# First two batches interleaved, a new order in both sweeps, and new places for the first tiles of pass B

## The chip, the cores and the metric

One core of one Trainium2 chip runs the whole program. The metric is the device time of one execution in microseconds (us); lower is better. TensorE (PE) multiplies matrices into PSUM, VectorE (DVE), ScalarE (ACT) and GpSimd (POOL) work on tiles in SBUF, and SyncE (SP) issues all the DMAs, in one queue and in order. Each engine executes its own list of instructions in order and waits on semaphores for the others.

## The reference

Three layers over 8 batches of 576 rows follow each other: a linear attention, a mixer with a ReLU, and a gated unit with a tanh GELU.

```python
kv = einsum('bhsd,bhse->bhde', k, v); o = einsum('bhsd,bhde->bhse', q, kv)      # 8 heads of 64
x  = o / sqrt(mean(o*o) + 1e-6) * g_norm                                          # heads joined: 576 x 512
u  = x + (x^T @ U @ V)^T                                                          # rank 32 over the rows
z  = u + relu(u @ w_ch1) @ w_ch2                                                  # 512 -> 2048 -> 512
h  = gelu(z @ w_in); a, v = h[..., :512], h[..., 512:]
out = z + (a * (w_sg @ layernorm(v) * g_ln + b_sg)) @ w_out
```

## The kernel before, in words

Every product of fp32 values is made of three products of float32r tiles (`three`, L319): a value is split into a high tile (an ACT copy) and a low tile (a DVE or POOL subtraction). Weights come from DRAM as 64-bit pairs and are turned into fp32 first (`convert`, L95): two ACT instructions, three DVE instructions and one POOL addition for each, and then the two of the split.

**The first sweep** goes over the batches. For a batch, `att_kv` (K) multiplies keys and values of a pair of heads, `put_kv` copies the four results into the block diagonal tile `kvbd`, `att_x` (X0 to X4) multiplies the queries with it in five chunks of rows, `att_root` and `att_norm` normalize on DVE, `att_t` (T0 to T4) multiplies with U, and `att_u` (D0 to D3) transposes, adds the rank-32 part, writes u to DRAM and splits it. `ch1` (U) is one unit of the product u @ w_ch1 for the first six of the sixteen 128-wide columns of the hidden layer: 12 matmuls of 288 columns, 12 such units for a batch. PERIOD (L503) is written out by hand and says in which order PE does the units of batch b, K of batch b+2, and X, T, D of batch b+1; ahead of the first period stands a preamble (L445 to L501) that does all of attention for batch 0 and K for batch 1. `cook_1` and `cook_2` prepare the other ten columns' weights in the periods 1 to 5, after the units 4, 6 and 9 of a period.

**The second sweep** (`Unit`, L554) makes those ten columns in a Strassen-like form with seven products for a block of 1024 rows (five blocks). Each product ends in an ACT or DVE instruction that reads its PSUM tile (`keep`, `result`); `after` (L606) puts the next block's loads, sums and splits (`split_t`) between them.

**Pass B** reads relu(y) back (`load_y`, L695: a DMA, an ACT relu to `yh`, a DVE instruction to `yl`) and multiplies it with w_ch2 (`ch2`); each step takes one tile `yr`. The third layer follows.

PE's order is written by hand. The other engines' order is made by a scheduler from the order of the program and a priority (a counter, which `later(n)` raises by n), except where `behind` keeps two instructions in program order. A tile's place is set by pool and tag: a tag with `bufs=2` alternates between two places, and a new tile waits until the old one's readers are done. The preamble's keys and values have two places (`kvm`, `kvr`), so the loads of pairs 2 and 3 wait for K of pairs 0 and 1. The pool `cp` holds the five prepared weights c0 to c4, each written by `cook_2` in the periods 1 to 5.

Of the kernel before, what the change touches and what calls it, by code (L numbers as in the profile page):

```python
# [12 lines left out]
F32 = mybir.dt.float32  # L13
F32R = mybir.dt.float32r
# [7 lines left out]

B, H, S, D = 8, 8, 576, 64
DM, DFF, RANK = 512, 2048, 32
EH = 512
P = 128
NP = H // 2
# [31 lines left out]
def tile_kernel(ctx: ExitStack, tc: tile.TileContext, kvm, kvr, qt, gcol, uv, w12,  # L59
# [102 lines left out]
    kv_t, q_t = {}, {}  # L162

    def load_kv(b, p):
        m = ap.tile([P, 4, 2 * P], F32, tag="kvm", bufs=2, name="kvm")
        r = ap.tile([S - 4 * P, 2 * P], F32, tag="kvr", bufs=2, name="kvr")
        nc.sync.dma_start(m, kvm[b, p])
        nc.sync.dma_start(r, kvr[b, p])
        kv_t[b, p] = (m, r)

    def load_q(b, p):
        q = ap.tile([P, S], F32, tag=f"q{p}", name=f"q{p}")
        nc.sync.dma_start(q, qt[b, p])
        q_t[b, p] = q
# [32 lines left out]
    def cook_2(i):  # L207
# [8 lines left out]
        for o, x in ((slice(0, 2), a[:, 0:2]), (slice(2, 3), a[:, 3:4]), (slice(3, 7), s)):  # L216
            behind(nc.scalar.activation(c[:, 0, o], x, AF.Copy))
            behind(nc.vector.tensor_sub(c[:, 1, o], x, c[:, 0, o].bitcast(F32)))

    at_s = {}  # L220

    def att_kv(b, ps):
        if ps[0] == 0:
            at_s["kv", b] = pm.tile([P, NP, D], F32, tag="ar", bufs=4, name="kvps")
        acc = at_s["kv", b]
        for p in ps:
            m, r = kv_t.pop((b, p))
            for c in range(NC):
                src = m[:, c] if c < 4 else r
                for j in range(2):  # L230
                    mm(acc[j * D:(j + 1) * D, p, :], src[:, j * D:(j + 1) * D],
                       src[:, P + j * D:P + (j + 1) * D], start=(c == 0), stop=(c == NC - 1))
# [7 lines left out]
    def att_x(b, c):  # L240

        n = rows(c)
        if c == 0:
            at_s["ss", b] = ap.tile([P, NC, H], F32, tag="ss", name="ss")
            nc.gpsimd.memset(at_s["ss", b][64:, 4], 1.0)
        ps = pm.tile([P, H, D], F32, tag="ar", bufs=4, name="xps")
        for p in range(NP):
            mm(ps[:n, 2 * p:2 * p + 2, :], q_t[b, p][:, c * P:c * P + n], kvbd[:, p, :],  # L248
               start=True, stop=True)
        xn = ap.tile([P, H, D], F32, tag=f"xn{c}", name="xn")  # L250
        sq = ap.tile([P, H, D], F32, tag="sq", name="sq")
        nc.scalar.activation(sq[:n], ps[:n], AF.Square)
        nc.scalar.activation(xn[:n], ps[:n], AF.Copy)
        nc.vector.tensor_reduce(at_s["ss", b][:n, c], sq[:n], AX.X, ALU.add)
        at_s["x", b, c] = xn

    def att_root(b):
        ss = at_s.pop(("ss", b))
        y, t = (ap.tile([P, NC, H], F32, tag=i, name=i) for i in ("ny", "nt"))
        a, y2, t2 = (i.rearrange("p w h -> p (w h)") for i in (ss, y, t))  # L260
        nc.vector.tensor_scalar(a, a, 1.0 / D, EPS, ALU.mult, ALU.add)
        in_turn(rsqrt(y2, t2, a))
        at_s["y", b] = y
# [178 lines left out]

    nu = NC * RANK
    cut = nu + HS
    for p in range(2):  # L445
        load_kv(0, p)
    nc.gpsimd.memset(kvbd, 0.0)
    make_identity(nc, ident)
    for p in range(2):
        att_kv(0, [p])  # L450
        load_kv(0, p + 2)
    for p in range(NP):
        load_q(0, p)
    for p in range(2, NP):
        att_kv(0, [p])
    put_kv(0)
    uvr = [slot(8 + h, [w, 2], I32, "uv") for h, w in enumerate((cut, HS))]
    for h in range(2):
        nc.sync.dma_start(uvr[h].rearrange("p n k -> p (n k)"), uv[:, 2 * cut * h:2 * cut + 2 * HS * h])
    nc.sync.dma_start(g, gcol)  # L460
    for f in range(2):
        load_w(f, 0)
    for p in range(2):
        load_kv(1, p)
    for f in range(2, 4):
        load_w(f, 0)
    for c in range(NC):
        att_x(0, c)
    for p in range(NP):
        load_q(1, p)  # L470
    tmp_u = next_tmp()[:, :nu]
    in_turn(convert(uvr[0][:, :nu], tmp_u))
    store_u(tmp_u)
    att_root(0)
    att_norm(0, (0, 1))
    tmp_v = [next_tmp()[:, :HS] for _ in range(2)]
    for h, (r, t) in enumerate(zip((uvr[0][:, nu:], uvr[1]), tmp_v)):
# [2 lines left out]
    for cs in ((0, 1), (2, 3), (4,)):  # L480
        if cs[0]:
            att_norm(0, cs)
        for c in cs:
            att_t(0, c)
    for p in range(2):
        att_kv(1, [p])
        load_kv(1, p + 2)
    split_w(0)
    split_w(1)
    for d in range(ND):  # L490
        att_u(0, d)
    for p in range(2, NP):
        att_kv(1, [p])
    put_kv(1)
    for p in range(2):
        load_kv(2, p)
    for f in range(4, NA):
        load_w(f, 0)
    for f in range(2, NA):
        split_w(f)  # L500
    flush()  # L501

    PERIOD = "X0 X1 X2 X3 U U X4 U U K0 U K1 U T0 T1 U T2 T3 U T4 U K2 U K3 U U D0 D1 D2 D3".split()  # L503
    for b in range(B):
        n, n2 = (i if i < B else None for i in (b + 1, b + 2))
        i = 0
        if n is None:
            at.close()
            px["xa"] = xa = pha.enter_context(tc.tile_pool(name="xa", bufs=1, side="right", reuse_waits="tile"))
            first_block()  # L510
        for s in PERIOD:
            c = int(s[1:] or 0)
            if s[0] == "U":
                ch1(b, i)
                i += 1
                if 1 <= b <= NI and i in (4, 6, 9):
                    if i < 9:
                        cook_1(b - 1, i // 2 - 2)
                    else:
                        cook_2(b - 1)  # L520
                if b < NI and i in (10, 11):
                    load_w(NA + 2 * b + i - 10, 0)
            elif s[0] == "K" and n2:
# [82 lines left out]
    def after(j, i, p):  # L606


        if j + 1 < len(BLOCKS):
            if 1 <= i < 4:  # L610
                at_ = done[j] = done.get(j, -1) + 1
                if at_ == 0:
                    load_blocks(j + 1)
                elif at_ in (6, 8, 10):
                    sums(j + 1, {6: "T1", 8: "T2", 10: "T3"}[at_])
                elif at_ in (12, 13):
                    split_t(j + 1, {12: "T1", 13: "B11"}[at_])
            if i == NI - 1 and p != 4 and p != 2:
                w = {5: "B22", 1: "T2", 3: "T3", 6: "B21", 7: "T4"}[p]
                if w == "T4":  # L620
                    sums(j + 1, w)
                split_t(j + 1, w)
            if j + 2 < len(BLOCKS) + 1 and p == 4 and i < 4:
                f = 4 * j + i
                if f == 0:
                    load_w(0, 1, 18)
                split_w2(f)
                if f + 1 < NF:
                    load_w(f + 1, 1, 18)
        elif p == 4 and i == 0:  # L630
            flush()
# [40 lines left out]
    p2["rw"] = ph1.enter_context(tc.tile_pool(name="rw", bufs=1, side="right", reuse_waits="tile"))  # L672
    bp = ph1.enter_context(tc.tile_pool(name="bp", bufs=1, side="left", reuse_waits="tile"))
    pm1 = ph1.enter_context(tc.tile_pool(name="pm1", bufs=1, space=PSUM, reuse_waits="tile"))
    tmps[:] = [bp.tile([P, DM], F32, tag=f"tmp{i}", name=f"tmp{i}") for i in range(2)]

    HOMES = (8, 9, 10, 11, 12, 13, 0, 1, 2, 3, 4, 5)
    wio_raw, wio = {}, {}
# [14 lines left out]
        nc.sync.dma_start(zt[b], ud[b])  # L693

    def load_y(j, i):  # L695
        y = bp.tile([P, 2, BT], F32, tag="y", bufs=3, name="yr")
        nc.sync.dma_start(y, yd[j][:, 2 * i:2 * i + 2])
        yh = bp.tile([P, 2, BT], F32R, tag="yh", bufs=2, name="yh")
        yl = bp.tile([P, 2, BT], F32R, tag="yl", bufs=2, name="yl")
        nc.scalar.activation(yh, y, AF.Relu)  # L700
        nc.vector.scalar_tensor_tensor(yl, y, 0.0, yh.bitcast(F32), ALU.max, ALU.subtract)  # L701
        for k in range(2):
            ys[j, 2 * i + k] = yh[:, k], yl[:, k]
# [328 lines left out]
```

## Time and profile before

| | us |
|---|---|
| median of 3 runs (1418.52 to 1425.31) | 1422.9 |
| the profiled execution | 1419.69 |
| its span, first to last instruction | 1417.7 |
| PE busy (8050 matmuls) | 1353.7, 95% |
| DVE busy | 768.2, 54% |
| ACT busy | 544.8, 38% |
| POOL busy | 280.4, 20% |
| mean granted TensorE clock | 0.985 |

How to read it: PE is the engine that has the most to do, so what counts is where PE has nothing to do, and where a matmul takes longer than elsewhere. In the page's 40 slices PE has 5, 8, 8 and 8 tenths or more in the first ones (35 us each), 7 in the slice around 570 us, and 8 or 9 in nearly all others.

### The profile page before, as it was taken

To read this page: it belongs to the slowest core of one execution; us is meant where nothing else is said; L and a number is where in the kernel's file an instruction comes from. 1 tells how busy PE (TensorE), PEld (TensorE's weight loads), DVE (VectorE), ACT (ScalarE), POOL (GpSimd) and SP (SyncE) were. 2 spreads that over 40 slices of the span, in tenths; PEclk is the share of its full clock that TensorE was granted. 3 is DMA by queue.
4 is the path that set the end of the run, shared out by engine and by line. 5 is a ranking of instruction groups with operands and counts; after the bars stand their busy time and mean duration, and the time that the engine had idled before them with its cause. 6 is when DMAs were issued, how large, how long until landed. Compare 5 with 4: busy or idle time off the path is not lost.

```text
span 1417.7 us, 20709 instructions
## 1 busy us (share of the span) xinstructions
PE 1353.7 (95%) x8050; PEld 1180.6 (83%) x8050; DVE 768.2 (54%) x1373; ACT 544.8 (38%) x920; POOL 280.4 (20%) x268
## 2 busy tenths in 40 slices
PE   5889999999999899699999999999999999999998
PEld 3788888888778788588888888888999999999998
DVE  3746666646566653232223232556775775865864
ACT  3756666654444442221212121444432423333321
POOL 1400000000110110200000000326253543533332
PEclk8899999999999999899999999999999999999999
DMA  7666665445666677834454543741020110211001
GB/s 247 205 190 209 204 213 184 148 144 184 213 229 226 213 259 258 310 93 130 130 170 157 170 140 120 245 134 57 1 68 18 51 50 18 68 34 34 34 17 51
DMA packets 86929, 199.43 MB, mean 141 GB/s; under 512 B 12208, under 2 KB 33456, under 8 KB 85040
## 3 DMA queue, kind: packets, MB, share of 16 engines
q1 hardware_dynamic: 86832, 198.12, 42.0%
q8 instruction: 63, 1.03, 0.3%
q14 instruction: 34, 0.28, 0.1%
HBM read 126.00 MB, written 72.09 MB: 140 GB/s over the span
## 4 chain that ended last, share of the span: by engine, by line
PE 76%; DVE 6%; DMA 6%; ACT 3%; issue 2%; POOL 1%; SPq 1%; DVEq 0%; ACTq 0%; POOLq 0%
PE acc L321 9%; PE acc L322 9%; PE acc L320 9%; PE uso L883 8%; PE uso L904 5%; PE uso L795 4%; PE c L320 3%; PE c L321 3%; PE c L322 3%; PE y L320 2%; PE y L322 2%; PE y L321 2%; PE xps L248 2%; DMA zl<-zd 2%; PE v L320 2%
## 5 line engine op out<-in xcount | busy, mean ns | idle before, releaser
L320 PE MATMUL acc<-yh,w 128*128 128x512 f32 x576 | 225.5, 392 | 10.3 <-ACT yh L700 10.3
L701 DVE SCALAR_TENSOR_TENSOR yl<-yr,yh 128x1024 fp32r<-128x1024 f32 x72 | 89.4, 1241 | 258.4 <-ACT yh L700 258.1
L321 PE MATMUL acc<-yl,w 128*128 128x512 f32 x576 | 225.6, 392 | 0.6 <-DVE yl L701 0.5
L322 PE MATMUL acc<-yh,w 128*128 128x512 f32 x576 | 225.3, 391 | 0.0
L700 ACT ACTIVATE yh<-yr 128x1024 fp32r<-128x1024 f32 x72 | 76.4, 1061 | 284.8 <-PE acc L322 271.8
L320 PEld LDWEIGHTS acc<-yh,w 128*128 128x128 f32 x576 | 108.8, 189 | 32.9 <-ACT yh L700 10.5
L321 PEld LDWEIGHTS acc<-yl,w 128*128 128x128 f32 x576 | 108.7, 189 | 24.2 <-DVE yl L701 1.5
L322 PEld LDWEIGHTS acc<-yh,w 128*128 128x128 f32 x576 | 108.8, 189 | 22.5
L320 PE MATMUL c<-uh,w 128*128 128x288 f32 x384 | 118.0, 307 | 1.8 <-ACT y L337 1.3
L321 PE MATMUL c<-ul,w 128*128 128x288 f32 x384 | 114.0, 297 | 0.8 <-DVE ul L317 0.8
L322 PE MATMUL c<-uh,w 128*128 128x288 f32 x384 | 113.6, 296 | 0.0
L795 PE MATMUL uso<-zh,wio 128*128 128x288 f32 x512 | 94.2, 298 | 1.2 <-DVE g2u L803 1.2
L904 PE MATMUL uso<-gh,wio 128*128 128x288 f32 x512 | 93.1, 296 | 0.0
L108 POOL TENSOR_TENSOR tmp<-tmp,raw 128x512 int32<-128x512 int32 x22 | 33.6, 1528 | 270.4 <-DVE tmp L107 256.0
L320 PE MATMUL y<-T,c 128*128 128x512 f32 (+1 forms) x200 | 75.5, 378 | 9.6 <-DVE y L568 9.4
L108 POOL TENSOR_TENSOR tmp<-tmp,wior 128x512 int32<-128x512 int32 x12 | 15.7, 1306 | 345.8 <-DVE tmp L107 300.8
L904 PEld LDWEIGHTS uso<-gh,wio 128*128 128x128 f32 x512 | 78.0, 189 | 2.3 <-issue 0.2
L795 PEld LDWEIGHTS uso<-zh,wio 128*128 128x128 f32 x512 | 76.4, 188 | 3.8 <-PE uso L883 1.8
L320 PEld LDWEIGHTS c<-uh,w 128*128 128x128 f32 x384 | 72.7, 189 | 5.5 <-ACT y L337 1.5
L322 PE MATMUL y<-T,c 128*128 128x512 f32 (+1 forms) x200 | 74.7, 373 | 0.0
L321 PEld LDWEIGHTS c<-ul,w 128*128 128x128 f32 x384 | 72.7, 189 | 2.3 <-DVE ul L317 1.2
L321 PE MATMUL y<-T,c 128*128 128x512 f32 (+1 forms) x200 | 74.5, 372 | 0.0
(178 smaller groups left out, 2963.5 us busy)
## 6 DMA issues: line engine op xcount, KB each, us to landing
yr<-yd SPq DMA_DIRECT2D x72, 512.0 KB, 3.7
yd<-y SPq DMA_DIRECT2D x92, 256.0 KB, 3.2
kvm<-kvm_dram SPq DMA_DIRECT2D x32, 512.0 KB, 4.4
raw<-w_dram SPq DMA_DIRECT2D x32, 512.0 KB, 4.4
q<-qt_dram SPq DMA_DIRECT2D x32, 288.0 KB, 5.2
ud<-ut SPq DMA_DIRECT2D x32, 288.0 KB, 2.1
z<-ud SPq DMA_DIRECT2D x8, 1152.0 KB, 6.4
out_dram<-ot SPq DMA_DIRECT2D x31, 288.0 KB, 2.1
```

Source lines behind the costliest of these rows:

```text
L108: yield behind(nc.gpsimd.tensor_add(t, t, low))
L248: mm(ps[:n, 2 * p:2 * p + 2, :], q_t[b, p][:, c * P:c * P + n], kvbd[:, p, :], start=True, stop=True)
L320: mm(ps, ah, bh, start=start, stop=False, **kw)
L321: mm(ps, ah, bl, start=False, stop=False, **kw)
L322: mm(ps, al, bh, start=False, stop=stop, **kw)
L700: nc.scalar.activation(yh, y, AF.Relu)
L701: nc.vector.scalar_tensor_tensor(yl, y, 0.0, yh.bitcast(F32), ALU.max, ALU.subtract)
L795: mm(ps[:, e, :HS], a[:, s], c[:, halves[e]], start=(d == 0 and i == 0), stop=(d == ND - 1 and i == 2))
L883: mm(ps[:, e, :HS], a[:, s], w[:, halves[e]], start=(c == 0 and i == 0), stop=(c == NC - 1 and i == 1))
L904: mm(ops[d][:, e, :HS], a[:, s], c[:, f, halves[e]], start=(f == 0 and i == 0), stop=(f == ND - 1 and i == 2))
```

## The change

It has six parts, told in the order of the program.

1. The five places of `cp` are allocated at the start as `spare` tiles. Keys and values of the pairs 2 and 3 of batches 0 and 1 land in `spare[2]` and `spare[3]`, the raw weights of the columns 0 to 5 in `spare[0]` and `spare[1]`, and batch 0's normalized rows and small tiles live in `spare[4]`. All eight loads of batch 0 and its queries are now issued without a wait for PE.
2. The preamble does all four K of batch 0, X of batch 0, all four K of batch 1, and then T of batch 0 and X of batch 1 in turns. The root of batch 1 follows D of batch 0. The weights 2 to 5 are split later: 2 and 3 before the first period, 4 and 5 inside it.
3. The first period (FIRST) has no X any more.
4. In PERIOD, X4 comes after one unit instead of two, T2 after two units instead of one behind T1, T4 after two instead of one, and D after one instead of two.
5. In the second sweep the splits that stand at the end of a block get a priority that is later by 25.
6. In pass B three `yr` tiles and the two tiles `yx` (which hold `yh` and `yl` together) are allocated before and after the `tmp` tiles, at other places than before.

```diff
     def load_kv(b, p):
-        m = ap.tile([P, 4, 2 * P], F32, tag="kvm", bufs=2, name="kvm")
-        r = ap.tile([S - 4 * P, 2 * P], F32, tag="kvr", bufs=2, name="kvr")
+        if b < 2 and p >= 2:
+            x = spare[2 + b][:, (p - 2) * 5 * 2 * P:(p - 1) * 5 * 2 * P].rearrange("p (c k) -> p c k", c=5)
+            m, r = x[:, :4], x[:S - 4 * P, 4]
+        else:
+            m = ap.tile([P, 4, 2 * P], F32, tag="kvm", bufs=2, name="kvm")
+            r = ap.tile([S - 4 * P, 2 * P], F32, tag="kvr", bufs=2, name="kvr")
...
     def load_w(f, h, at_=None):
+        if f < NA and h == 0:
+            w_raw[f, h] = spare[f // 3][:, f % 3 * 2 * DM:(f % 3 + 1) * 2 * DM].bitcast(I32).rearrange(
+                "p (n k) -> p n k", k=2)
+            load_pairs(w_raw[f, h], w12[f], h)
+            return
...
-    for p in range(2):
+    for p in range(NP):
         load_kv(0, p)
+    for p in range(NP):
+        load_q(0, p)
...
-    for p in range(2):
-        att_kv(0, [p])
-        load_kv(0, p + 2)
...
+    att_kv(0, list(range(NP)))
     put_kv(0)
...
+    att_root(0)
     tmp_u = next_tmp()[:, :nu]
     in_turn(convert(uvr[0][:, :nu], tmp_u))
     store_u(tmp_u)
-    att_root(0)
+    att_kv(1, list(range(NP)))
+    put_kv(1)
     att_norm(0, (0, 1))
...
         for c in cs:
             att_t(0, c)
+        for c in cs:
+            att_x(1, c)
...
+    att_root(1)
+    for p in range(NP):
+        load_q(2, p)
+    split_w(2)
+    att_norm(1, (0, 1))
+    split_w(3)
+
+    PERIOD = "X0 X1 X2 X3 U X4 U U K0 U K1 U T0 T1 U U T2 T3 U U T4 U K2 U K3 U D0 D1 D2 D3".split()
+    FIRST = "U U U K0 U K1 U T0 T1 U U T2 T3 U U T4 U K2 U K3 U D0 D1 D2 D3".split()
...
+                if b == 0 and i in (1, 3, 5):
+                    if i < 5:
+                        split_w(4 + i // 2)
+                    else:
+                        flush()
...
-                if w == "T4":
-                    sums(j + 1, w)
-                split_t(j + 1, w)
+                with later(LATER):
+                    if w == "T4":
+                        sums(j + 1, w)
+                    split_t(j + 1, w)
...
+    y_at = [bp.tile([P, 2, BT], F32, tag="y", bufs=3, name="yr")]
     tmps[:] = [bp.tile([P, DM], F32, tag=f"tmp{i}", name=f"tmp{i}") for i in range(2)]
+    yx_at = {i: bp.tile([P, 2, 2, BT], F32R, tag=f"yx{i}", name="yx") for i in (1, 0)}
```

What this makes of the engines' lists shows at three places. The first is PE in the preamble, behind X of batch 0; `tp` is the result of T, `kvps` of K, `xps` of X, `ups` of D. Before, T stands alone:

```order
L248 MATMUL xps<-kvbd,q_171 64x128
L286 MATMUL tp<-xh,u_118 128x512
L288 MATMUL tp<-xl,u_118 128x512
...
L286 MATMUL tp<-xh,u_118 128x512
L231 MATMUL kvps<-kvm 64x64 x8
L231 MATMUL kvps<-kvr 64x64 x2
...
L310 MATMUL ups<-ident,xn 128x128 x2
```

The same place now (`spare_126` holds keys and values of batch 1, `q_260` a query tile of batch 1):

```order
L255 MATMUL kvps<-kvr 64x64 x2
L255 MATMUL kvps<-spare_126 64x64 x20
L310 MATMUL tp<-xh,u_118 128x512
L312 MATMUL tp<-xl,u_118 128x512
...
L272 MATMUL xps<-kvbd,q_260 128x128
L272 MATMUL xps<-kvbd,q_262 128x128
```

K of batch 1 has moved ahead of T of batch 0, and two chunks of X of batch 1 stand behind T0 and T1, two behind T2 and T3, and the last behind T4.

The second is DVE in a steady period (batch 1), from the low part of the last normalized chunk (`xh<-xn,xh 64x512`) to the copy into `kvbd`; `t` is the tile that D multiplies, `sums` and `c` belong to `cook_2`. Before:

```order
L277 TENSOR_TENSOR xh<-xn,xh 64x512
L292 TENSOR_TENSOR t_1224<-tp,t_1224 32x512
L212 TENSOR_TENSOR sums_1242<-pair_1096 128x256
L213 TENSOR_TENSOR sums_1242<-sums_1242,pair_1096 128x256
L214 TENSOR_TENSOR sums_1242<-pair_1096 128x256
L215 TENSOR_TENSOR sums_1242<-pair_1096,sums_1242 128x256
```

Now:

```order
L301 TENSOR_TENSOR xh<-xn,xh 64x512
L222 TENSOR_TENSOR sums_1221<-pair_1094 128x256
L223 TENSOR_TENSOR sums_1221<-sums_1221,pair_1094 128x256
L224 TENSOR_TENSOR sums_1221<-pair_1094 128x256
L225 TENSOR_TENSOR sums_1221<-pair_1094,sums_1221 128x256
L228 TENSOR_TENSOR c_1222<-pair_1094,c_1222 128x512
L228 TENSOR_TENSOR c_1222<-pair_1094,c_1222 128x256
L228 TENSOR_TENSOR c_1222<-sums_1221,c_1222 128x1024
L316 TENSOR_TENSOR t_1234<-tp,t_1234 32x512
```

The seven instructions of `cook_2` have moved ahead of the low part of `t`.

The third is DVE at the end of a block of the second sweep; `T` is a split tile of the next block, `y<-` a result that frees a PSUM tile. Before:

```order
L640 TENSOR_TENSOR w_4054<-tmp_3762,w_4054 128x512
L423 TENSOR_TENSOR T_4140<-tf,T_4139 128x1024
L423 TENSOR_TENSOR T_4153<-q,T_4152 128x1024
L568 TENSOR_TENSOR y<-y,s_4162 128x512
L568 TENSOR_TENSOR y<-y,m_4094 128x512
```

Now:

```order
L665 TENSOR_TENSOR w_4037<-tmp_3745,w_4037 128x512
L447 TENSOR_TENSOR T_4123<-tf,T_4122 128x1024
L592 TENSOR_TENSOR y<-y,s_4145 128x512
L592 TENSOR_TENSOR y<-y,m_4077 128x512
L447 TENSOR_TENSOR T_4136<-q,T_4135 128x1024
```

One split, T from q, has moved behind two results.

## Rows read from the trace of the kernel before

**Rows 1.** Busy time by stretch: us, engines (instructions), granted clock, DMA share, GB/s.
```profile
0.00:100.00 100.00, 73.71 (x582) 62.00 (x583) 52.93 (x102) 51.28 (x103) 18.65 (x24) 0.88 0.66 220
330.00:420.00 90.00, 84.81 (x359) 66.85 (x358) 51.93 (x68) 39.95 (x67) 11.12 (x7) 1.00 0.61 204
420.00:570.00 150.00, 140.11 (x693) 116.94 (x691) 80.79 (x116) 61.56 (x112) 14.05 (x9) 0.99 0.71 243
```
**Rows 2.** Timeline of SP and PE, the start: us, duration, instruction, idle before.
```profile
9.05 2.01 SPq L173 DMA_DIRECT2D q<-qt_dram  x4
...
16.66 5.86 PE L248 MATMUL xps<-kvbd,q 128*128 128x128 f32 x34 [0.46 <-DMA q<-qt_dram]
29.57 0.80 PE L286 MATMUL tp<-xh,u 128*128 128x512 f32 x1 [7.05 <-ACT xh L276]
51.81 3.81 PE L248 MATMUL xps<-kvbd,q 128*128 128x128 f32 x32 [1.01 <-ACT raw L103]
55.38 0.38 PE L320 MATMUL c<-uh,w 128*128 128x288 f32 x1
58.73 1.09 PE L248 MATMUL xps<-kvbd,q 128*64 128x128 f32 x8
73.53 0.50 PE L286 MATMUL tp<-xh,u 128*128 128x512 f32 x1 [3.44 <-ACT xh L276]
```
**Rows 3.** Timeline of DVE in the preamble: t, and the last low part of u.
```profile
40.08 0.70 DVE L292 TENSOR_TENSOR t<-tp,t 32x512 fp32r<-32x512 f32 x1 [1.66 <-ACT t L291]
51.74 0.76 DVE L317 TENSOR_TENSOR ul<-ut,uh 128x576 fp32r<-128x576 f32 x1
```
**Rows 4.** Busy time in a stretch of the preamble; the granted clock is the third last number.
```profile
30.00:39.00 9.00, 4.98 (x9) 2.30 (x8) 6.66 (x14) 3.68 (x9) 3.54 (x3) 0.50 0.01 4
```
**Rows 5.** Chain that ended last: start us, us; X0 of batches 2, 3 and 4.
```profile
94.47 0.91 PE xps L248 x8
131.56 3.57 PE xps L248 x32
168.09 3.57 PE xps L248 x32
```
**Rows 6.** PE's waits, 100 to 330 us (total, times, longest), and one wait.
```profile
PE tp L288 <- DVE xl L277: 6.7, 10, 0.9
...
151.62 0.50 PE L288 MATMUL tp<-xl,u 128*128 128x512 f32 x1 [0.84 <-DVE xl L277]
```
**Rows 7.** Timeline of DVE in a period: first and last of `cook_2`'s instructions.
```profile
156.62 0.42 DVE L212 TENSOR_TENSOR sums<-pair 128x256 f32<-128x256 f32 x1
159.31 1.23 DVE L218 TENSOR_TENSOR c<-sums,c 128x1024 fp32r<-128x1024 f32 x1 [0.19 <-ACT c L217]
```
**Rows 8.** Timeline of ACT and POOL: first and last instruction for one weight.
```profile
65.01 0.68 ACT L102 ACTIVATE tmp<-raw 128x512 f32<-128x512 f32 x1 [1.42 <-POOL w L125]
69.83 1.26 POOL L125 TENSOR_TENSOR w<-tmp,w 128x512 fp32r<-128x512 f32 x1 [0.74 <-ACT w L124]
```
**Rows 9.** Timeline of DVE and PE at two block ends of the second sweep.
```profile
485.71 2.32 DVE L423 TENSOR_TENSOR T<-tf,T 128x1024 fp32r<-128x1024 f32 x1
487.95 1.21 DVE L423 TENSOR_TENSOR T<-q,T 128x1024 fp32r<-128x1024 f32 x1
489.09 0.68 DVE L568 TENSOR_TENSOR y<-y,s 128x512 f32<-128x512 f32 x1
...
386.61 0.50 PE L320 MATMUL y<-T,c 128*128 128x512 f32 x1 [2.58 <-DVE y L568]
489.82 0.51 PE L320 MATMUL y<-T,c 128*128 128x512 f32 x1 [3.70 <-DVE y L568]
```
**Rows 10.** Timeline of SP, ACT and PE: the first tiles of pass B.
```profile
568.89 0.92 SPq L697 DMA_DIRECT2D yr<-yd  x2
576.17 1.06 ACT L700 ACTIVATE yh<-yr 128x1024 fp32r<-128x1024 f32 x1 [8.68 <-DMA yr<-yd]
577.28 0.79 PE L320 MATMUL acc<-yh,w 128*128 128x512 f32 x1 [10.25 <-ACT yh L700]
```

More of the change, by code (lines that the diff above doesn't have):

```diff
@@ L24 @@
 DM, DFF, RANK = 512, 2048, 32
+LATER = 25
 EH = 512
@@ L218, in cook_2, with xn_of, small @@
             behind(nc.vector.tensor_sub(c[:, 1, o], x, c[:, 0, o].bitcast(F32)))
+    spare = [cp.tile([P, 7 * DM], F32, tag=f"c{i}", name=f"spare{i}") for i in range(NI)]
+    def xn_of(b, c):
+        if b:
+            return ap.tile([P, H, D], F32, tag=f"xn{c}", name="xn")
+        return spare[4][:, c * DM:(c + 1) * DM].rearrange("p (h d) -> p h d", h=H)
+    def small(b, name, i):
+        if b:
+            return ap.tile([P, NC, H], F32, tag=name, name=name)
+        o = NC * DM + i * NC * H
+        return spare[4][:, o:o + NC * H].rearrange("p (c h) -> p c h", c=NC)
     at_s = {}
@@ L243, in att_x @@
         if c == 0:
-            at_s["ss", b] = ap.tile([P, NC, H], F32, tag="ss", name="ss")
+            at_s["ss", b] = small(b, "ss", 0)
             nc.gpsimd.memset(at_s["ss", b][64:, 4], 1.0)
@@ L249, in att_x @@
                start=True, stop=True)
-        xn = ap.tile([P, H, D], F32, tag=f"xn{c}", name="xn")
+        xn = xn_of(b, c)
         sq = ap.tile([P, H, D], F32, tag="sq", name="sq")
@@ L258, in att_root @@
         ss = at_s.pop(("ss", b))
-        y, t = (ap.tile([P, NC, H], F32, tag=i, name=i) for i in ("ny", "nt"))
+        y, t = (small(b, n, i) for i, n in ((1, "ny"), (2, "nt")))
         a, y2, t2 = (i.rearrange("p w h -> p (w h)") for i in (ss, y, t))
@@ L444, in tile_kernel @@
     cut = nu + HS
-    for p in range(2):
+    for p in range(NP):
         load_kv(0, p)
+    for p in range(NP):
+        load_q(0, p)
     nc.gpsimd.memset(kvbd, 0.0)
     make_identity(nc, ident)
-    for p in range(2):
-        att_kv(0, [p])
-        load_kv(0, p + 2)
[L452 to L455, printed above, removed]
+    att_kv(0, list(range(NP)))
     put_kv(0)
@@ L460, in tile_kernel @@
     nc.sync.dma_start(g, gcol)
-    for f in range(2):
-        load_w(f, 0)
-    for p in range(2):
+    for p in range(NP):
         load_kv(1, p)
-    for f in range(2, 4):
-        load_w(f, 0)
+    load_w(0, 0)
     for c in range(NC):
@@ L470, in tile_kernel @@
         load_q(1, p)
+    for f in range(1, NA):
+        load_w(f, 0)
+    att_root(0)
     tmp_u = next_tmp()[:, :nu]
@@ L484, in tile_kernel @@
             att_t(0, c)
+        for c in cs:
+            att_x(1, c)
     for p in range(2):
-        att_kv(1, [p])
-        load_kv(1, p + 2)
+        load_kv(2, p)
     split_w(0)
@@ L491, in tile_kernel @@
         att_u(0, d)
[L492 to L503, printed above, removed]
+    att_root(1)
+    for p in range(NP):
+        load_q(2, p)
[4 more added lines that the diff above has]
+    FIRST = "U U U K0 U K1 U T0 T1 U U T2 T3 U U T4 U K2 U K3 U D0 D1 D2 D3".split()
     for b in range(B):
@@ L510, in tile_kernel @@
             first_block()
-        for s in PERIOD:
+        for s in PERIOD if b else FIRST:
             c = int(s[1:] or 0)
@@ L695, in load_y @@
     def load_y(j, i):
-        y = bp.tile([P, 2, BT], F32, tag="y", bufs=3, name="yr")
+        y = y_at.pop() if y_at else bp.tile([P, 2, BT], F32, tag="y", bufs=3, name="yr")
         nc.sync.dma_start(y, yd[j][:, 2 * i:2 * i + 2])
-        yh = bp.tile([P, 2, BT], F32R, tag="yh", bufs=2, name="yh")
-        yl = bp.tile([P, 2, BT], F32R, tag="yl", bufs=2, name="yl")
+        k = i % 2
+        yx = yx_at.pop(k) if k in yx_at else bp.tile([P, 2, 2, BT], F32R, tag=f"yx{k}", name="yx")
+        yh, yl = yx[:, 0], yx[:, 1]
         nc.scalar.activation(yh, y, AF.Relu)
```

## The prediction

> **What bounds the kernel now.** I read the busy time by stretch first [rows 1]: PE is busy for 73.71 of the first 100 us, at a granted clock of 0.88, and for 84.81 of 90 and 140.11 of 150 us in the second sweep; nearly everywhere else it has no hole. So the end is set by PE, and a change can only gain what PE loses in holes, or what it loses at the lower clock. Then the waits and the timeline of PE in those stretches. In the preamble PE ends X of batch 0 and stands 7.05 us until the first normalized tile is there; it starts the first unit at 55.38 and stands 3.44 us again before T of batch 1 [rows 2]. From 30 to 39 us its granted clock is 0.50, the lower of its two levels (1.2 of 2.4 GHz) [rows 4]. In the steady periods the reader sees one repeated wait, of T2 and T3 for the low tile `xl`: 6.7 us in ten waits, five periods with two each, 0.84 the larger of a pair [rows 6]. In the second sweep PE stands 2.58 and 3.70 us at two block ends, for a DVE result that frees a PSUM tile [rows 9]. At the start of pass B it stands 10.25 us until ScalarE has the first `yh`, which in turn waits for the load of `yr` [rows 10].
>
> **The preamble.** Before, the loads of keys and values of pairs 2 and 3 wait for PE, and the queries stand behind them in SP's queue and go out at 9.05 [rows 2]. Now eight loads go out without a wait, and the queries behind them as the first ones land, which could be at most some 4 us earlier; the same bytes have to arrive, so I take about 3 us at X. From there DVE is the path: root, norm, the low tiles. There I add what is new in its list, the copy into `kvbd` for batch 1 ahead of the first low tile, and the reduces of X of batch 1 between the norms: about 1 us. So the low part of `t`, at 40.08 before [rows 3], I put at 38.
>
> From there to the last low part of u, before, DVE needs 52.5 (51.74 + 0.76) - 40.08 = 12.4 us [rows 3], and that holds the conversion of weights 0 and 1, and the copy into `kvbd`. Now the copy is done earlier, but three reduces, the root of batch 1 and a norm stand in between, while ScalarE has the copies of X of batch 1 among its own: I take 12 us, plus 2 for what stalls and ScalarE's turn add. That gives 52 to 53, the same as before. So the low parts of u gain nothing. But what comes next differs: before, PE then does X of batch 1 (51.81) and starts the units at 55.38 [rows 2]; now X is done and the first unit can end half a microsecond after the last low part, as if it had begun at 52.2.
>
> The period from there, at the upper clock: a steady one takes 168.09 - 131.56 = 36.5 us [rows 5], less X (3.57 us for 32 of its 40 matmuls [rows 5], so 4.5 for all), less the pair of waits (1.3), makes 30.7. Before, the first period took 94.47 - 55.38 = 39.1 us [rows 2, 5] and held one chunk of X (1.0), so it lost 39.1 - 1.0 - 30.7 = 7.4 to waits and to the clock. What will it lose now? The wait of 3.44 us for T of batch 1 goes, since its root stands ahead of the units. In its place weight 1 is late: its low half on POOL stands behind the conversion of weight 2, which DVE does after the last low part of u. One weight takes 71.09 - 65.01 = 6.1 us from the first ScalarE instruction to the end of POOL's subtraction (69.83 + 1.26) [rows 8]; I count about 3 us that PE stands before the third unit. And PE comes out of a stretch with holes, so the first units run at the lower level: 2 us. I take 4.7, between 0 and the 7.4 of before.
>
> So X of batch 2 starts at 52.2 + 30.7 + 4.7 = 87.6 instead of 94.47: **-6.9 us**. Ends: 52.2 + 30.7 less 1 is -12.6; 3 us later with a loss of 7.4 is -1.2.
>
> Here the Trainium skill speaks against the change. The rows show X of batch 0 at 5.86 us for 34 matmuls [rows 2] and X of batch 3 at 3.57 for 32 [rows 5], 0.17 against 0.11 us each, so early X runs at the lower level. TensorE: Matmul & The Clock Gate, section What's actually happening, says that "the default state is throttled, and activity releases the throttle". By that rule X of batch 1, moved ahead into a stretch with holes, loses the upper level that it has before (3.81 us at 51.81 [rows 2]) and takes 40 x 0.17 = 6.8 instead of 4.5; by the rows these 2.3 us lie beside DVE's and ScalarE's chain and cost nothing in my sum.
>
> **The steady periods.** Two units instead of one stand between T1 and T2, so T2 comes one unit later against DVE, and a unit is longer (two take 58.73 - 55.38 = 3.35 us, so one 1.7 [rows 2]) than the 0.84 of the wait [rows 6]. X4 and T0 keep their distance. Five periods with 1.3 us each: **-6.6 us**. What is late next: `cook_2` now stands before the low part of `t` on DVE, 160.54 - 156.62 = 3.9 us [rows 7], and D behind it has one unit less of cover. Counting DVE and ScalarE from T2 on, `t` is there about 2.8 us before D asks for it. Ends: -6.6 and 0.
>
> **The second sweep.** At both block ends a split of 2.32 us and one of 1.21 stand ahead of the result that PE waits for (489.09 behind 487.95) [rows 9]. Only the one of 1.21 moves behind it; the longer one stays. So 2.58 becomes 1.4 and 3.70 becomes 2.5: 2.4 us, and some tenths elsewhere, where results come ahead of a conversion: **-3 us**. The tiles whose splits are moved are used late in the next block. Ends: -5 and +1.
>
> **Pass B.** The two first loads of `yr` stand at the same place of SP's queue as before, behind the last result's write and three loads of weights, and `yh` starts when `yr` lands, 7.3 us after its issue (576.17 - 568.89) [rows 10]. Other places in SBUF do not change that: **0**. Ends: -4, if it was in truth a wait for the place, and +1.
>
> **The sum.** 6.9 + 6.6 + 3 = 16.5 off the profiled execution's 1419.7 makes 1403.2. The median of the runs shown lies 3.2 above that execution; I forecast 1404, within that spread.
>
> **The rivals.**
>
> The first period is paced by the weights. Weights 2 to 5 were split ahead of it and are now split inside; if each pair of units waits for a whole weight, 6.1 us [rows 8] instead of two units of some 1.7, it costs 6 x (6.1 - 3.4) = 16 us in place of the 4.7: 1403.2 + 11.5 = 1414.7, and about 1417 with the lower clock. For it: the chain over three engines is long and two `tmp` tiles bound it. Against it: DVE's list leaves room, and T, K and D stand between the units.
>
> D waits for `cook_2`. This one ends on the other side. If the low part of `t` comes after PE has reached D, PE stands in five periods. At the full 3.9 us, with the clock falling after it, as it is at the lower level around the holes of the preamble [rows 4], I price 3.9 + 1.7 = 5.6 each, 28 in all: 1431. It decides from 2.8 us of lateness on, and outweighs the gains from 16.5 / 5 = 3.3 us a period. For it: DVE's list has been turned round exactly there. Against it: the margin.
>
> T's wait does not go but moves to `xl` of another chunk, since two places for `xh` bind it to PE's progress: 1403.2 + 6.6 = 1410. For it: the wait is with DVE, whose work is not less.
>
> The preamble gives all that is there, no loss in the first period: 1403.2 - 5.7 = 1397.5.
>
> The places of pass B do matter: 1403.2 - 4 = 1399. Against it: the load's own landing ends the wait [rows 10]. Otherwise this part does not do what it says.
>
> **How the numbers follow.** My forecast 60%; weights pace 10%; T's wait stays 10%; the preamble gives more 10%; pass B 6%; D waits 4%. The forecast's own ends are 1398 to 1410. The range has to hold the cases of 1397 and of 1410, and a part of the 1415: 1395 to 1414. A difference of 0.5% (7.1 us) is about what a measurement of this kernel can tell. Faster by more, below 1415.8: all but the weights' case and D's, with something off for what I have not seen, 0.85; within it 0.11; slower 0.04.
>
> **What would show it.** Right: X of batch 2 at about 87 us; no wait of 3.44 before T of batch 1, but one before the third unit; no pair of waits at T2 and T3 in the periods 1 to 5; two block ends with about 1.4 and 2.5; the hole before pass B still some 10 us. Wrong: X of batch 2 after 93 or before 83; a wait of PE at D for `t`; the hole before pass B shorter than 8 us.

## The result, and the profile after

The kernel after takes 1406.3 us (median of 4 runs, 1404.1 to 1407.8) where before takes 1423.1 (4 runs beside it, 1418.5 to 1425.3): a ratio of 0.9885, 95% interval 0.9857 to 0.9913. Forecast were 1404.0 us and 1395 to 1414. The profiled execution went from a span of 1417.7 to 1404.8 us: 12.9 us, which the ledger below takes apart. The medians differ by 16.8, because the profiled execution of before (1419.7 us) lies 3.4 under its median and that of after 0.6 over it.

The windows of the kernel after answer to [rows 1] (columns as there), and one more to the stretch around the first units:

```profile
0.00:100.00 100.00, 77.06 (x616) 66.55 (x616) 54.55 (x112) 54.01 (x109) 20.98 (x24) 0.90 0.66 226
330.00:420.00 90.00, 86.35 (x366) 68.58 (x367) 59.04 (x77) 40.55 (x65) 10.82 (x7) 1.00 0.65 218
420.00:570.00 150.00, 132.44 (x650) 109.75 (x649) 72.29 (x106) 57.62 (x106) 14.84 (x9) 0.95 0.72 249
50.00:60.00 10.00, 6.62 (x25) 5.34 (x24) 8.19 (x18) 5.12 (x10) 3.67 (x4) 0.64 0.79 253
```

The third window is not better than before: it now holds the whole hole ahead of pass B. Fixed windows mislead where work has moved; the ledger at the same points of the program does not. The chain that ended last (start, us) has X0 of batch 2 and X of batch 7, after and then before:

```profile
89.95 0.91 PE xps L272 x8
265.24 3.57 PE xps L272 x32
```
```profile
277.83 3.57 PE xps L248 x32
```

The timeline of PE has the first product of the second sweep and the last one, after and then before:

```profile
317.89 0.40 PE L344 MATMUL x<-T,c 128*128 128x512 f32 x1
554.44 0.28 PE L346 MATMUL y<-T,c 128*128 128x256 f32 x1
```
```profile
329.67 0.40 PE L320 MATMUL x<-T,c 128*128 128x512 f32 x1
566.74 0.28 PE L322 MATMUL y<-T,c 128*128 128x256 f32 x1
```

| Point of the program | before | after | gained by then | gained here |
|---|---|---|---|---|
| X0 of batch 2 | 94.47 | 89.95 | 4.5 | preamble 4.5 |
| X of batch 7 | 277.83 | 265.24 | 12.6 | five periods 8.1 |
| first product, second sweep | 329.67 | 317.89 | 11.8 | last period -0.8 |
| last product, second sweep | 566.74 | 554.44 | 12.3 | second sweep 0.5 |
| first matmul, pass B | 577.28 | 564.80 | 12.5 | hole 0.2 |
| end of the span | 1417.7 | 1404.8 | 12.9 | 0.4 |

PE's timeline after, from T0 of batch 0 over the third unit and T3 of batch 1 to the two block ends and pass B, answers to [rows 2, 9, 10]:

```profile
28.11 0.77 PE L310 MATMUL tp<-xh,u 128*128 128x512 f32 x1 [4.26 <-DVE u L370]
60.74 0.61 PE L346 MATMUL c<-uh,w 128*128 128x288 f32 x1 [2.85 <-POOL w L126]
74.69 0.50 PE L312 MATMUL tp<-xl,u 128*128 128x512 f32 x1 [0.79 <-DVE xl L301]
373.39 0.50 PE L344 MATMUL y<-T,c 128*128 128x512 f32 x1 [1.28 <-DVE y L592]
475.59 0.50 PE L344 MATMUL y<-T,c 128*128 128x512 f32 x1 [2.32 <-DVE y L592]
564.80 0.79 PE L344 MATMUL acc<-yx,w 128*128 128x512 f32 x1 [10.08 <-ACT yx L728]
```

In the periods 1 to 5 the pair of waits of [rows 6] is gone. The wait of 3.44 us before T of batch 1 is gone too; one of 2.85 for weight 1 stands in its place.

### The profile page after: what moved, and what is told of

Read it like the earlier page. It is cut to its first block, busy times and chain, and to the rows that moved or that the text cites. A ratio compares the mean times of both kernels' runs of the same rounds, so it can differ in the third digit from the quotient of the medians.

```text
span 1404.8 us, 20707 instructions
## 1 busy us (share of the span) xinstructions
PE 1350.7 (96%) x8050; PEld 1180.4 (84%) x8050; DVE 763.5 (54%) x1373; ACT 544.6 (39%) x920; POOL 285.6 (20%) x268
## 4 chain that ended last, share of the span: by engine, by line
PE 80%; DMA 5%; DVE 5%; ACT 3%; issue 1%; POOL 1%; SPq 0%; DVEq 0%; ACTq 0%; POOLq 0%
PE acc L345 9%; PE acc L346 9%; PE acc L344 9%; PE uso L911 8%; PE uso L932 6%; PE uso L823 5%; PE c L344 4%; PE c L346 3%; PE c L345 3%; PE y L344 2%; PE y L346 2%; PE y L345 2%; PE v L344 2%; PE v L345 2%; PE v L346 2%; PE xps L272 2%
## 5 line engine op out<-in xcount | busy, mean ns | idle before, releaser
L344 PE MATMUL acc<-yx,w 128*128 128x512 f32 x576 | 225.0, 391 | 10.1 <-ACT yx L728 10.1
L729 DVE SCALAR_TENSOR_TENSOR yx<-yr,yx 128x1024 fp32r<-128x1024 f32 x72 | 90.2, 1254 | 257.6 <-ACT yx L728 257.1
L345 PE MATMUL acc<-yx,w 128*128 128x512 f32 x576 | 225.1, 391 | 1.5 <-DVE yx L729 1.5
L346 PE MATMUL acc<-yx,w 128*128 128x512 f32 x576 | 224.6, 390 | 0.0
L728 ACT ACTIVATE yx<-yr 128x1024 fp32r<-128x1024 f32 x72 | 76.4, 1061 | 284.9 <-PE acc L346 272.0
L344 PEld LDWEIGHTS acc<-yx,w 128*128 128x128 f32 x576 | 108.5, 188 | 33.0 <-ACT yx L728 10.3
L345 PEld LDWEIGHTS acc<-yx,w 128*128 128x128 f32 x576 | 108.5, 188 | 25.0 <-DVE yx L729 2.5
L346 PEld LDWEIGHTS acc<-yx,w 128*128 128x128 f32 x576 | 108.5, 188 | 22.4
L344 PE MATMUL y<-T,c 128*128 128x512 f32 (+1 forms) x200 | 75.7, 379 | 9.7 <-DVE y L592 7.9
L344 PEld LDWEIGHTS c<-uh,w 128*128 128x128 f32 x384 | 73.6, 192 | 3.8 <-issue 1.0
L109 POOL TENSOR_TENSOR tmp<-tmp,raw 128x512 int32<-128x512 int32 x16 | 25.7, 1604 | 249.3 <-DVE tmp L108 230.0
L346 PEld LDWEIGHTS c<-uh,w 128*128 128x128 f32 x384 | 73.7, 192 | 3.1 <-POOL w L126 3.1
L346 PE MATMUL y<-T,c 128*128 128x512 f32 (+1 forms) x200 | 74.6, 373 | 0.0
```

What stands on the lines that cost most here:

```text
L109: yield behind(nc.gpsimd.tensor_add(t, t, low))
L344: mm(ps, ah, bh, start=start, stop=False, **kw)
L345: mm(ps, ah, bl, start=False, stop=False, **kw)
L346: mm(ps, al, bh, start=False, stop=stop, **kw)
```

## Experiments

Runs of one kernel differ by 1 to 7 us, so single microseconds are read from the trace at the points above. These have a spread too, since each kernel was profiled once. By the timeline (0.16 ahead of the chain) X0 of batch 2 starts at 89.8 to 91.1 us in eight profiles with the same preamble (the kernel after is the earliest), as X of batch 0 starts at 13.1 to 13.8. The second sweep takes 235.3 to 237.4 us in five profiles with the code of the kernel after for it (the kernel after itself, the old order, the old places, weight 1 first, the later copy).

**The order of a period, undone.**

```
-    PERIOD = "X0 X1 X2 X3 U X4 U U K0 U K1 U T0 T1 U U T2 T3 U U T4 ...
+    PERIOD = "X0 X1 X2 X3 U U X4 U U K0 U K1 U T0 T1 U T2 T3 U T4 ...
```

> The kernel after with one line undone: a steady period is again in the order U U X4 ... T0 T1 U T2 T3, so one unit stands between T1 and T2 and two between X3 and X4. Theory: this order alone made the gain of the periods, 8.1 us over the five periods between X of batch 2 and X of batch 7 (35.0 us each after, 36.6 before). Then the pair of waits at T2 and T3 is back, a period is 36.6 us, and the time is about 1414 us, 8 above the kernel after. Rival: the waits went because the new preamble leaves DVE and ScalarE ahead of PE; then the periods stay at 35.0 us and the time at 1406.

1417.7 us (10 runs), ratio to before 0.9976 (0.9964 to 0.9988): 11.4 above the median after. Its waits and chain have the pair back, and 183.2 us between the two points that lie 175.3 apart after:

```profile
PE tp L312 <- DVE xl L301: 7.5, 11, 1.0
```
```profile
90.83 0.91 PE xps L272 x8
274.04 3.57 PE xps L272 x32
```

The rival falls: the order makes 7.9 of the gain in the five periods. The other 3.5 us are 0.9 of a later preamble, 0.8 in the last period, and the rest in small parts later. The time lies 3.7 above the expected 1414.

**The order alone, in the kernel before.** The same line the other way.

> The kernel before with one line changed: the new order of a steady period, for the first period too. Theory: the order alone gives 36.6 - 35.0 = 1.6 us in each of five periods and about 1 in the last, the wait of 3.4 us for T of batch 1 in the first period becomes shorter too: 8 to 12 us, 1409 to 1413. Rival: without the new preamble DVE is further behind and the pair of waits at T2 and T3 only moves: at most 3 us, 1418 or more.

1414.2 us, 0.9945 (0.9924 to 0.9966). The periods are 35.1 us, the gain there is 8.1 without the new preamble. The time is just outside the expected 1409 to 1413: X0 of batch 2 comes at 98.2, 3.8 later than before, and the wait for T of batch 1, expected shorter, is 4.45 instead of 3.44. Most of the 3.8 lies ahead of the first thing that the edit moves: the first unit starts at 58.80 instead of 55.38, behind an X of batch 1 that took 5.93 us instead of 3.81. The granted clock from 50 to 58 us was 0.53 here and 1.00 in the profile before. So two profiles of the old preamble differ by 3.4 us at the first unit, and the ledger's 4.5 us for the new one is taken from the quicker of the two.

```profile
53.12 5.93 PE L248 MATMUL xps<-kvbd,q 128*128 128x128 f32 x32 [1.00 <-issue]
58.80 0.38 PE L320 MATMUL c<-uh,w 128*128 128x288 f32 x1
74.79 0.79 PE L286 MATMUL tp<-xh,u 128*128 128x512 f32 x1 [4.45 <-ACT xh L276]
98.23 0.91 PE xps L248 x8
```

**No shift of the splits: `LATER = 0`.**

> The kernel after with LATER = 0: the splits at a block end of the second sweep are no longer put behind the results. Theory: the waits of PE at the two block ends go from 1.28 and 2.32 back to about 2.6 and 3.7 us, but the 1.82 us that PE waits for ScalarE at 539.93 goes back to what it was, since what was gained there only met the slow writes of the results earlier: the end of the sweep moves by less than 1 us, and the time is 1406 to 1407.5. Rival, as the prediction had it: the splits give 3 us at the end of the sweep, and this kernel takes 1409.

1406.9 us, 0.9899 (0.9884 to 0.9914). The two waits at the block ends are back at 2.40 and 3.41 us, yet from first to last product the sweep takes 236.2 us, against 236.6 after. As the theory had it: the shift takes 1.1 us out of each of two waits and nothing out of the sweep that exceeds the spread. The sum of PE's waits there tells why: 11.9 us before, 11.1 after, 11.0 without the shift. What the two block ends gave came back elsewhere, for instance as 0.60 us at 497.77, where the result that PE waits for now stands behind a weight's conversion. The waits of the sweep by what ended them, after and then without the shift (total, times, longest):

```profile
PE y L344 <- DVE y L592: 7.9, 8, 2.3
PE y L344 <- ACT m L585: 1.8, 1, 1.8
PE x L344 <- ACT m L585: 1.4, 2, 1.2
```
```profile
PE y L344 <- DVE y L592: 8.1, 5, 3.4
PE x L344 <- ACT m L585: 2.9, 3, 1.6
```

The two block ends without the shift:

```profile
374.44 0.50 PE L344 MATMUL y<-T,c 128*128 128x512 f32 x1 [2.40 <-DVE y L592]
477.54 0.50 PE L344 MATMUL y<-T,c 128*128 128x512 f32 x1 [3.41 <-DVE y L592]
```

**A fifth place for results.**

```
-            y = m2.tile([P, BT], F32, tag="y", bufs=4, name="y")[:, :self.n]
+            y = m2.tile([P, BT], F32, tag="y", bufs=5, name="y")[:, :self.n]
```

> The kernel after with five places instead of four for the results of the second sweep. Theory: what the moved splits gained at the block ends did not reach the end of the sweep because ScalarE, at 538.43, waits 2.7 us for a result's place that is still being written to DRAM, and the next pair's copies stand behind it, for which PE waits 1.82 and 1.18 us: with a fifth place these two waits go to under 1 us together, the sweep ends 2 us earlier, and the time is about 1404. Rival: the writes themselves are the bound, five places are full as four were; the waits move by a unit and the time stays at 1406.

1405.6 us, 0.9883 (0.9864 to 0.9903); the sweep takes 236.4 us. The waits for copies add up to 2.2 instead of 3.2 us, and the end does not move: a fifth place is no cure. The rival fits, though nothing here shows more than that ScalarE, idle for 8.16 us, is still let go by the write to DRAM:

```profile
538.04 0.38 ACT L594 ACTIVATE y<-y 128x256 f32<-128x256 f32 x1 [8.16 <-DMA yd<-y]
```

**An OR on DVE instead of POOL's addition.**

```
-        yield behind(nc.gpsimd.tensor_add(t, t, low))
+        if add:
+            yield behind(nc.gpsimd.tensor_add(t, t, low))
+        else:
+            yield behind(nc.vector.tensor_tensor(t, t, low, ALU.bitwise_or))
...
-        in_turn(convert(w_raw.pop((f, 1)), next_tmp()))
+        in_turn(convert(w_raw.pop((f, 1)), next_tmp(), False))
```

(`add` is a new parameter, false for the second weights alone.)

> The kernel after, where the last step of the conversion of the second weights, an integer addition on POOL (1.64 us each), is an OR on DVE instead (it leaves out the carry of the rounding). Theory: the split of 2.33 us that stands ahead of the result at a block end is a split of 1.21 to 1.25 us that DVE and POOL do beside each other: the addition on POOL starts at 472.22, the split at 472.61. Without POOL the split takes 1.25, the OR about 0.7, and the waits of PE at the two block ends go from 1.28 and 2.32 to about 0.8 and 1.9 us. Rival: the split is long because of where its operands lie, or because ScalarE writes the next tile's high part at the same time; then it keeps its 2.3 us, and the waits grow by the OR to about 2.0 and 3.0 us. Either way the time stays within 1 us of 1406.

1398.7 us, 0.9841 (0.9815 to 0.9868). The mechanism is the theory's, its worth far more than I gave it. DVE and POOL in the kernel after, at the second block end:

```profile
472.61 2.33 DVE L447 TENSOR_TENSOR T<-tf,T 128x1024 fp32r<-128x1024 f32 x1
474.86 0.68 DVE L592 TENSOR_TENSOR y<-y,s 128x512 f32<-128x512 f32 x1
```
```profile
472.22 1.63 POOL L109 TENSOR_TENSOR tmp<-tmp,raw 128x512 int32<-128x512 int32 x1 [7.11 <-DVE tmp L108]
```

The same place with the OR (L112):

```profile
467.88 0.68 DVE L112 TENSOR_TENSOR tmp<-tmp,raw 128x512 int32<-128x512 int32 x1
469.08 1.22 DVE L450 TENSOR_TENSOR T<-tf,T 128x1024 fp32r<-128x1024 f32 x1
470.21 0.68 DVE L595 TENSOR_TENSOR y<-y,s 128x512 f32<-128x512 f32 x1
```

The split drops from 2.33 to 1.22. Its overlap with POOL was 473.85 - 472.61 = 1.24, and 2.33 - 1.22 = 1.11 is nearly that: DVE stood. So says the Trainium skill, SBUF — State Buffer, Who interferes with whom: a DVE instruction with two inputs in SBUF and a GpSimd one that reads SBUF exclude each other for a whole instruction; the trace agrees. The rest of the sweep after says the same, and against the rival's ScalarE: the splits of 128x1024 that no addition on POOL overlaps take 1.21 to 1.23 us, the one at 407.92 too, beside which ScalarE writes the next high part; those that it overlaps are longer by about the overlap (at 370.39 1.27 and a split of 2.35, at 464.72 0.39 and 1.47).

```profile
407.92 1.23 DVE L447 TENSOR_TENSOR T<-q,T 128x1024 fp32r<-128x1024 f32 x1 [3.31 <-ACT T L446]
408.26 1.06 ACT L446 ACTIVATE T<-tf 128x1024 fp32r<-128x1024 f32 x1
```

The sweep takes 544.99 - 318.29 = 226.7 us, 9.9 less than after and 8.6 to 10.7 less than the five profiles above. PE's waits in it fall from 11.1 to 3.7; both block ends are without one. Part of the rest is the clock after a hole, first after, then with the OR (the third last number):

```profile
476.00:486.00 10.00, 10.00 (x38) 7.98 (x37) 6.68 (x10) 2.73 (x5) 0.00 (x0) 0.83 0.85 298
```
```profile
476.00:486.00 10.00, 10.00 (x45) 8.03 (x44) 7.29 (x13) 7.12 (x13) 0.00 (x0) 1.00 0.77 286
```

PE is busy throughout in both, with 38 matmuls recorded against 45. The hole does not bring this loss each time: the variant with the old places stands 2.29 us there and stays at 1.00.

**Pass B's first tiles in their old places.** The set-aside tiles and the joint tag are undone.

> The kernel after with the first tiles of pass B in the places that they had before (no tile set aside ahead of the conversion's, two tags for the high and the low part). Theory: the hole of PE before pass B is set by the landing of the first load of yr, 7.1 us after its issue, whichever place it goes to: the hole stays at 10 us and the time at 1406. Rival: the places let the first load or the first high part start earlier; then the hole grows to 14 us and the time to about 1410.

1407.7 us, 0.9909 (0.9893 to 0.9924). Pass B starts at 564.84 instead of 564.80, after a hole of 10.84 us (10.08 after). The part does nothing that exceeds the spread.

**Weight 1 first.** One `flush()` ahead of `split_w(2)`.

> The kernel after with the high and low part of weight 1 written ahead of the conversion of weight 2 (one call more, ahead of it). Theory: the 2.85 us that PE waits before the third unit is the low part of weight 1 on POOL, which stands behind the conversion's addition for weight 2; now it goes ahead, the wait is under 0.5 us, X of batch 2 starts at about 87.3 instead of 89.8, and the time is about 1403.5. Rival: the weights come one after the other through three engines in any case, so weight 2 is late by as much and PE waits 2 to 3 us before the fifth unit instead: no change, 1406.

In the trace the theory holds: the wait before the third unit is gone, the next one for a weight is 0.40 us, and X0 of batch 2 is at 87.03, though the last low part of u comes 1.0 us later (54.32 for 53.29).

```profile
87.03 0.91 PE xps L272 x8
```

The runs don't tell it: 1406.1 us, 0.9891 (0.9876 to 0.9906), 1404.05 in the profiled one.

**The copy into `kvbd` later.** `put_kv(1)` behind `att_norm(0, (0, 1))`.

> The kernel after with the copy of batch 1 into kvbd behind the first two normalized tiles and the low part of the U factor, instead of ahead of them. Theory: in the preamble DVE is the path, and this copy is the reason that the low part of t came at 39.1 us and not at 38: PE's wait for T of batch 0 goes from 4.3 to about 3.4 us, X of batch 2 starts 0.5 to 1 us earlier, the time is about 1405.5. Rival: X of batch 1, which needs the copy, comes later by as much and the norms of batch 1 with it: X of batch 2 stays where it is, 1406.

1408.3 us, 0.9903 (0.9876 to 0.993). Nothing gained, but not the clean test that I wanted: the list now has the two low tiles ahead of the factor's low part too, T0 waits 4.95 us for that, and `t` comes at 40.38.

**One early tile for pass B.** The edit's core, behind the last pair but one:

```
+            if b.i == 1:
+                y0 = slot(5, [2, BT], F32, "yr")
+                nc.sync.dma_start(y0, yd[0][:, 8:10])
+            else:
+                yh, yl = (slot(6 + k, [2, BT], F32R, "yx") for k in range(2))
```

> The kernel after, with the first yr tile of pass B and its high and low part in slots 5, 6 and 7, which are free during the last units; loaded with the weights 8 to 11 and split behind the last pair of units. The weights 13, 14 and 15 go to slots 13, 9 and 8 in their place, once the last unit has done with the tiles there, and the later users of these slots change places with them. Theory: the hole of 10 us before pass B is one load's way, issue behind the last result's write and landing 7 us later; with the tile there, PE waits only until a PSUM tile is free, the hole is 1 to 2 us, and the time is about 1398. Rival: what ends the hole is next in line only by little (the weights, the second yr tile, the conversions on ScalarE): the hole stays over 5 us, or comes back within the first two steps of pass B, and the time is 1402 to 1406.

1410.2 us, 0.9913 (0.9888 to 0.9938), slower than the kernel after. The hole is gone, as the theory said (last product 555.12, first of pass B 555.24), and the rival takes it all back:

```profile
565.09 0.79 PE L344 MATMUL acc<-yx,w 128*128 128x512 f32 x1 [4.09 <-ACT yx L737]
577.66 0.51 PE L344 MATMUL acc<-yx,w 128*128 128x512 f32 x1 [3.42 <-ACT yx L737]
```

The first of these waits is for the second tile, whose load is issued at 557.27; the third tile's is issued at 568.94, behind six more weights and five pieces of wsg.

**The loads in the order of use.** Two early tiles; then:

```
-    load_y(*steps[0])
...
+    load_y(*steps[1])
+    load_y(*steps[2])
     load_z1(0)
-    load_y(*steps[1])
     for f in range(8):
         load_w2(f)
-    raws = prepare_sg()
...
+        if at_ == 4:
+            raws = prepare_sg()
```

> The kernel after with the first two yr tiles of pass B loaded early, into slots 5 and 4 (the first one's high and low part into 6 and 7), the weights 12 to 15 into slots 10, 13, 9 and 8 in their place, the third tile's load ahead of the weights 0 to 7 and of wsg, and the loads of wsg three steps later. Theory: what the variant with one early tile gained at the start of pass B (10 us) it lost to the next two tiles, which came behind eight weights and five pieces of wsg in SP's queue (waits of 4.1 and 3.4 us, and the clock at 0.73 and 0.84 of full in the two stretches of 10 us with them); with these two tiles ahead, the waits of the first three steps are under 2 us together, the hole before pass B stays away, and the time is 1397 to 1400. Rival: the DMA queues are full there (411 GB/s from 560 to 570 us in that variant), the same bytes have to arrive, and the wait only moves to a weight (12 or 13, at the third step): 1404 or more.

1396.0 us, 0.9818 (0.979 to 0.9846): 10 us under the kernel after. PE's waits for high and low parts at the start of pass B add up to 3.3 us (expected: under 2), against 9.5 with one early tile, and the granted clock from 555 to 575 is 1.00 instead of 0.74, with more bytes moved:

```profile
555.00:575.00 20.00, 16.80 (x70) 12.78 (x69) 3.66 (x3) 4.20 (x4) 0.00 (x0) 1.00 1.03 403
```
```profile
555.00:575.00 20.00, 9.73 (x34) 7.53 (x35) 2.45 (x2) 4.81 (x7) 1.94 (x2) 0.74 0.98 364
```

(The first is this variant, the second the kernel after.) The queues are as full as the rival had it; what counts is which bytes come first. Two things changed at once, the order in the queue and how early the first two tiles and the last four weights are asked for; no run parts them.

**All three edits.**

> The three edits together: weight 1 written ahead of the conversion of weight 2, the last step of the second weights' conversion as an OR on DVE (it leaves out the carry of the rounding), and the first tiles of pass B early and ahead of the weights. Theory: they act at different places (before the third unit, in the second sweep, at the start of pass B) and add up: 2.9 + 7.6 + 7 off 1406.3 makes 1388 to 1391. Rival: the second sweep ends 10 us earlier only to meet the same full DMA queues at the start of pass B, so that the second and third gain are one: 1394 to 1398.

1385.6 us, 0.9744 (0.9725 to 0.9763), 20.6 under the kernel after and below the expected 1388 to 1391. They add up: 2.9 by the trace, 7.6 and 10.3 by the runs make 20.8.

**And the OR in every conversion.**

> The combined kernel with the last step of every conversion as an OR on DVE (it leaves out the carry of the rounding), in the preamble, the periods and pass B too. Theory: in the preamble the additions on POOL stand in the chain to T of batch 0 and to the weights (2.31 and 2.71 us for the two that DVE works beside); without them the factor's copies come earlier, PE's waits before T0 and before the third unit get shorter, X of batch 2 starts 1 to 2 us earlier and the time is 1384 to 1385. Rival: DVE is the path of the preamble and gets 0.7 us more for each of six weights and two factors, and two more in each period, where its low tiles are what PE would wait for: 1386 to 1390.

1379.9 us, 0.971 (0.9694 to 0.9726), 26 under the kernel after, the fastest of all, 5.7 under the three edits and below the expected 1384 to 1385. Against those three, the last low part of u starts at 50.65 instead of 54.85, and X0 of batch 2 at 83.2 instead of 87.4, though `t` comes no earlier (39.69, and 39.21 with the additions). With the additions two DVE instructions on the way, beside which POOL works, take 1.51 and 1.29 us instead of 0.43 and 0.19. With the three edits, and then with the OR everywhere:

```profile
46.26 1.51 DVE L107 TENSOR_SCALAR tmp<-tmp 128x512 int32<-128x512 int32 x1
54.85 0.75 DVE L344 TENSOR_TENSOR ul<-ut,uh 128x576 fp32r<-128x576 f32 x1
```
```profile
45.79 0.43 DVE L107 TENSOR_SCALAR tmp<-tmp 128x512 int32<-128x512 int32 x1
50.65 0.75 DVE L341 TENSOR_TENSOR ul<-ut,uh 128x576 fp32r<-128x576 f32 x1
```

## Why the prediction was right, and where it was not

The time was right because the two larger terms stood on rows, and their errors cancelled in part. There was luck in it. Off the profiled execution the sum took 16.5 us and 12.8 came (1419.7 to 1406.9), 3.7 less; but the median after lies 0.6 under its profile, where before it lay 3.4 above, so that 1404 is missed by 2.3 only.

- **Preamble: forecast 6.9, measured 4.5** (3.2 to 4.5 by the eight profiles). The mechanism was as walked, the size off, in two terms.
  - The 3 us at X were right: it starts only 1.1 us earlier (14.19 to 13.06), behind K of the last pair and the copy into `kvbd`, but its matmuls end 3.2 earlier (22.5 to 19.3). The way from there to `t` was mis-sized: what is new in DVE's list cost 2.3 us, not about 1. The root ends 3.3 us earlier (24.82 for 28.13), but the last low part of a chunk starts only 1.0 earlier (36.76 for 37.73). In between now stand the conversion of the factor U (1.1 us in DVE's list; before, it ran in the root's gaps), the copy into `kvbd` (0.86) and a reduce (0.69). PE's wait of 4.26 us before T of batch 0 ends with the low part of U, which the prediction had not named. So `t` came at 39.1 instead of 38.
  - The last low part of u ended at 54.04 instead of 52 to 53. From there to X0 of batch 2 it took 35.9 us, forecast 34.6 to 35.6; the wait for weight 1 was 2.85 (forecast 3), and the clock was down, 0.64 from 50 to 60 us. In the sum itself 52.2 is too late by its own rows: a unit of 1.7 us that ends 0.5 behind 52.5 begins at 51.3. What held the last low part of u up is POOL's additions in part: without them it starts 4.2 us earlier. That another place for the copy into `kvbd` would give its share back isn't shown.
  - The size of the whole term is less sure than the ledger makes it. Against the slower profile of the old preamble it would be some 8 us; by the runs it is 3.4 with the old order (0.9976) and some 8 with the new one (1414.2 to 1406.3, other parts included).

```profile
13.06 6.25 PE L272 MATMUL xps<-kvbd,q 128*128 128x128 f32 x39 [1.08 <-issue]
26.59 0.86 DVE L262 COPY kvbd<-kvps 64x256 f32<-64x256 f32 x2
36.76 0.68 DVE L301 TENSOR_TENSOR xh<-spare,xh 64x512 fp32r<-64x512 f32 x1
```

- **Periods: 6.6, measured 8.1.** The pair of waits went, and a period fell from 36.7 to 35.1 us, 1.6 instead of the 1.3 that the waits show; the rest lies in gaps too short to be listed. D didn't wait for `cook_2`.
- **Second sweep: 3, measured 0.5.** This is the step that failed. The two waits shrank as forecast (1.28 and 2.32 for 1.4 and 2.5), but a shorter wait of PE was not a shorter sweep: without the shift the sweep is no longer. I took the split's 2.32 us as work, when half of it was DVE standing behind POOL. Taking POOL out gave 9.9 us. The 1.1 us twice did not arrive because PE's other waits in the sweep grew as these two shrank, 11.0 us in sum without the shift and 11.1 with it. Why just those grew is not settled: a fifth place was no help.
- **Pass B: 0, measured 0.2.** The places don't matter, and the landing of `yr` ends the hole, as [rows 10] had it. (The slice around 570 us has 6 tenths on the page before, not 7.) But it was no fixed price: in the order of use the same bytes hide beside the matmuls.
- The clock rule that I weighed against X of batch 1 didn't decide. X did run at the lower level at first: the first 16 of these matmuls took 3.51 us from 30.06 (granted clock 0.50 from 28 to 32 us), the next 16 then 1.95 from 34.34 (1.00), and with the last 8 it was 6.55 us in all, forecast 6.8 by that rule. The slow ones lay beside DVE's chain, for which PE still waited 1.22 us before T4 at 37.50. The 0.17 us for each of the early matmuls was a mixture: of the 34, the first 15 took 3.57 us, 0.24 each, and the others 0.12. The granted clock stands at 1.00 there, from 14 to 22 us, so that they ran at the lower level is not shown.

## What to carry to other kernels

An instruction's duration is not its work: where one shape takes 1.2 us in one place and 2.3 in another, look for the engine that ran beside it before moving the instruction. A hole that ends with a transfer is a matter of what stands ahead of it in the queue; move one load and the next takes its place, so put all of them in the order of use. A wait that shrinks counts only when the next fixed point of the program comes earlier.

## What the runs showed of the hardware that I had not expected

- POOL's integer addition on 128x512 (1.63 us) stretched a DVE subtraction beside it from 1.22 to 2.33 us. With the 16 additions done on DVE the sweep was 9.9 us shorter, though DVE was busier in it (137.0 us instead of 133.8).
- A hole of 2.32 us in an else busy PE was followed by 10 us at a granted clock of 0.83 with no hole in it. Its length doesn't decide alone: behind one of 2.29 us at the same place, in the variant with the old places, the clock stayed at 1.00.
- The first loads of pass B ran at 403 GB/s for 20 us (364 in the kernel after) beside a PE at a granted clock of 1.00.
